# A four-batch retention and Fourier-mixing kernel: the first batch's k read in long runs and transposed twice, under a new written order

## The chip, the cores and the metric

The kernel runs on one core of one Trainium2 chip. The metric is the device time of one execution in microseconds (us), lower is better. Inside the core TensorE multiplies matrices, VectorE, ScalarE and GpSimd do the element-wise work, and SyncE (SP) issues most of the DMAs. Each engine takes its own instructions in a fixed order and waits on semaphores for the others.

## What is computed

Two stages. The first is a recurrent linear attention with a decay per head, the second adds the real part of a two-dimensional Fourier transform, normalises each row, and applies a two-layer network. The cut reference:

```python
# q, k, v: (4 batches, 8 heads, 768 steps, 64) float32
gamma = 1.0 - 2.0 ** (-5.0 - np.arange(H))
for t in range(S):
    state = gamma * state + einsum('bhd,bhe->bhde', k[:, :, t], v[:, :, t])
    y[:, :, t] = 1 / sqrt(D) * einsum('bhd,bhde->bhe', q[:, :, t], state)
x = y.transpose(0, 2, 1, 3).reshape(B, S, H * D)          # (4, 768, 512)

mixed = real(fft(fft(x, axis=1), axis=2))
u = x + mixed
un = (u - mean(u)) / sqrt(var(u) + 1e-06)                  # over the last axis
out = u + maximum(un @ w_ch1, 0) @ w_ch2                   # 512 -> 2048 -> 512
```

## The kernel before

**How the work is cut.** The 768 steps of a head are six chunks of 128. Two heads make a pair, and the four pairs of a batch (taken in the order 0, 1, 3, 2) are one load each of q, k and v: 384 KB in float32, issued by `load_piece` (line 238) on SP. For the first batch q is read as `(p c)`: a partition holds six consecutive steps, which lie next to each other in memory as a run of 1536 bytes. k and v are read as `(c p)`: a partition holds step p of each chunk, in six runs of 256 bytes.

**The first batch, pair i.** `q{i}` casts q to float16 (line 450 and above), `k{i}0` and `k{i}1` cast the two heads of k and multiply with the decay to the end of the chunk (`gkd`), `v{i}0` casts v. `tq{i}` and `tk{i}` transpose q and k on TensorE, six 128x128 transposes each (line 468), `eq{i}` and `ek{i}` copy the result out of PSUM (line 480). As q stands in runs of six steps, `eq` writes with a stride, so that the steps are in order again; `ek` is a plain copy. `am{i}` multiplies the transposed k and q for half of the chunks, `ae{i}` masks the result into `atm` on VectorE (line 505). `kv{i}` multiplies k with v per chunk (line 516), `sc{i}` turns these into the running state with one scan on VectorE (line 529), `yi` and `yx` sum the part within the chunk and the part from the state, and `x{i}0`, `x{i}1` scale the two heads into the tile `x` (line 562).

**From x to the output.** The sequence is folded (`fs`, `fl`, `fh`, `fd`), multiplied with cosine and sine tables (`s1..`), copied out (`gc`, `gr`), multiplied with the tables of the other axis (`s2{kb}` for each of six row blocks), and `qn`, `ul`, `uu`, `xl`, `xu` build u. `bn` and `un` normalise. `ut` transposes a row block, on TensorE or, for later batches, with a transposing DMA on SP. `h` is the first layer into PSUM tiles named `psh` (lines 1101 and 1121; a pool of three), `r` its relu into `ht` (line 1111), `p` the second layer, `o` the last addition and `st` the store. For batches 1 to 3 the names carry the batch in front (`1tq0`, `2un3`, `3h0_1`); there `c..` casts the inputs (`cast_piece`, line 420, all on GpSimd), and r goes to ScalarE or VectorE by a table `ACT_ROWS`.

**What sets the order.** A text `ORDER` lists all units by name, some 1,360 of them, over all four batches. `play` issues them one after the other and `pin` chains each instruction to the one before it on its engine, so that each engine runs its instructions exactly in written order. Units named `f512` are filler matmuls on zeros that nobody reads. A second text, `ENGINES`, says for the first batch's small pieces which engine takes them: P is GpSimd, A ScalarE, D VectorE. The later batches' engines stand in the code. The weights are eight loads on GpSimd's queue (`w10` to `w23`), of which the first is held until the fourth pair's k has landed. Batch 1's first load waits for the seventh weight load and for the matmuls of `h13`.

Of the kernel before, what the change touches and what calls it, by code (L numbers as in the profile page):

```python
# [36 lines left out]
q0:P q1:P q2:P q3:P k00:P k01:P k10:P k11:P k20:A k21:P k30:P k31:A v00:P v10:P v20:A v30:P v31:A  # L37
eq0:D eq1:D eq2:A eq3:A ek00:D ek10:A ek20:A ek30:D ek31:D x00:A x01:A x10:A x11:A x20:A x21:A
x30:A x31:A tn0:D tn1:D tn2:A tn3:D tn4:D gk0:P gk1:A gk2:A gk3:A gc00a:A gc01a:A gc01b:D gc10a:A
gc11a:A gc11b:D ste0:D ste1:A xn0:P xn1:D cdh0:P cdh1:D nsp:P hid5:P fs0a:D fs0b:D fla:D flb:D  # L40
fha:D fhb:D fd0:D fd1:D gr0:P gr1:P gr2:D gr3:D nid0:D nid1:D hid:D
# [3 lines left out]
nid0 lq0 qtz00 lk0 pad01 qtz10 ta0 mp1 hid ta1 gk3 gk1 tn0 mp7 tb0 q0 tq0 tn1 tb1 si1 ab1 f512 mp5  # L45
k00 ab0 k01 tk0 par eq0 co0 ta2 tn2 f512 f512 f512 si0 ek00 am01 nid1 tb2 am00 ae011 ta3 lv0 v00
kv0 ae001 lq1 lk1 lv1 lq2 lk2 q1 tq1 tn3 tb3 k11 f512 f512 gk2 ab2 co2 qz0 si2 si3 ae010 yi01 eq1
gk0 lq3 k10 ae000 tk1 ek10 am10 sc0 lk3 lv2 ab3 yi00 yx0 f512 f512 x01 q2 ae101 v10 am11 ae110
ae111 k20 ae100 tq2 eq2 k21 tk2 ek20 x00 hid5 q3 mp2 kv1 sc1 k31 am21 yi10 nsp k30 am20 w10 w11
w12 ae210 ae201 yi11 yx1 ae200 ae211 tq3 x11 lv3 eq3 tk3 ek30 ek31 f512 ta4 am30 mp3 am31 tn4 tb4  # L50
f512 ae300 ae301 x10 fs0a f512 f512 f512 ae310 v20 kv2 sc2 si4 ab4 yi20 co4 yi21 co3 v31 f512 f512
yx2 v30 kv3 ae311 x20 fs0b s1s10 x21 sc3 flb cdh0 fla co1 fd0 yi31 yi30 yx3 w13 f512 x30 fd1 xn1
x31 xm0 close xm1 s1s00 w20 stx01 fha s1m0 gc00a s1m1 stx3 xn0 fhb s1s11 xmb gc11b gc10a g0a cdh1
s1s01 gc01a gc01b gr1 px1 w21 w22 gc11a gr3 stg00 stx4 stg01 stg10 stg11 stx2 ste1 s22 qn2 ste0
g0b g0c uu2 qe1 s21 qn1 mp0 gr0 ul2 xu2 gr2 uu1 mu1 xm2 mu2 h00 ul1 qz1 h02 un1 h01 s20 qn0 s23
qn3 ul0 xl2 uu0 xu0 s25 ut1 te1 ul3 xl3 h03 uu3 xu3 xl0 bn3 w23 h10 h13 1lk0 1lq0 qn5 uu5 ul5 xu5
un2 s24 qn4 ul4 h12 h11 xl5 ut2 te2 un3 bn5 0p0_1 1lv0 h22 h21 un5 xl4 1lq1 uu4 0p1_1 0p2_1 ut5
h20 ut3 half bn2 qtz01 xu4 bn4 un4 0rt1 1lk1 h23 0p0_0 0p1_0 1cq_0 1lv1 0p2_0 0p3_0 ut4 0p3_1
3ws21 1ck0_0 te5 bn0 te3 1lk2 bn1 0rt0 0rc0 1ck1_0 1tk0 1cv_0 1tq0 te4 1kv0_0 1s0_0 xe 0o1 1kv1_0
1s1_0 1lq2 1ck0_1 1lk3 0o0 1ek_0 0p0_2 1s2_0 1s3_0 1s4_0 0p1_2 0p2_2 1lv2 pad11 1eq1_0 1eq0_0  # L60
1a2_0 1m2_0 mp6 0h1_1 1cq_1 1tq1 1a1_0 0r1_1 1lq3 1eq1_1 1m1_0 0p3_2 0o2 1lv3 1ck1_1 1cv_1 1kv0_1
# [1446 lines left out]
```

## Time and profile before

| | |
|---|---|
| time, median of 3 runs | 239.75 us (238.5 to 240.43) |
| time of the profiled execution | 239.57 us |
| span of the profiled execution, first to last instruction | 237.9 us |
| busy time of VectorE, ScalarE, GpSimd | 190.8, 120.4, 90.9 us |
| DMA | 36.41 MB in 99,466 packets |
| mean granted TensorE clock | 0.993 |

The profile is of one execution. A busy share is time in which an engine has an instruction under way; for TensorE matmuls overlap, so the mean duration of one is longer than the step from one to the next. "Idle before" is the time an engine stood still before the instructions of a group, with what ended the wait. The chain of waits follows the last instruction back to what released it, step by step, and lists start, duration and what it was.

### The profile page before, as it was taken

How to read it: one execution, taken by the hardware profiler on the slowest of the kernel's cores; microseconds unless marked ns; L12 is line 12 of the kernel's file. 1: busy time of each engine (PE TensorE's matmuls, PEld its weight loads, DVE VectorE, ACT ScalarE, POOL GpSimd, SP SyncE). 2: the span in 40 equal slices, each digit the busy share in tenths (PEclk: the TensorE clock that was granted, in tenths of full speed). 3: DMA queues.
4: the chain of work that ended last, by engine and by line, in shares of the span. 5: the costliest groups of instructions: out<-in, count | busy, mean ns of one | idle time of the engine just before them, and what ended most of it. 6: DMA issues, size and time to landing. Idle time of an engine off the chain costs nothing.

```text
span 237.9 us, 5652 instructions
## 1 busy us (share of the span) xinstructions
PE 229.4 (96%) x2175; PEld 159.1 (67%) x2175; DVE 190.8 (80%) x484; ACT 120.4 (51%) x273; POOL 90.9 (38%) x149
## 2 busy tenths in 40 slices
PE   7889999999999999999999999899999999999994
PEld 2456899766776756665667556565666458888884
DVE  7959878878899799886999997987959784856374
ACT  7858875466887543445366334354155316142330
POOL 5667465446640098815404571600004504002302
PEclk9979999999999999999999999999999999999999
DMA  7999999999999999989999968704120240013222
GB/s 178 253 266 179 207 190 151 208 259 233 261 234 232 153 258 180 239 176 155 228 218 252 220 91 154 113 12 101 44 88 3 68 102 8 3 26 111 88 91 88
DMA packets 99466, 36.41 MB, mean 153 GB/s; under 512 B 89840, under 2 KB 96624, under 8 KB 99440
## 3 DMA queue, kind: packets, MB, share of 16 engines
q1 hardware_dynamic: 95072, 31.79, 66.0%
q0 software_dynamic: 4224, 4.19, 11.4%
q8 instruction: 17, 0.28, 0.5%
q14 instruction: 9, 0.07, 0.1%
q10 hardware_dynamic: 144, 0.07, 0.1%
HBM read 27.26 MB, written 6.29 MB: 141 GB/s over the span
## 4 chain that ended last, share of the span: by engine, by line
PE 87%; DMA 4%; DVE 4%; SPq 2%; issue 1%; POOL 1%; ACT 0%; DVEq 0%
PE psc L1146 26%; PE psh L1106 21%; PE psh L1192 8%; PE psc L1242 6%; PE psh L1128 5%; PE wkA L620 3%; PE ps L767 3%; DMA k<-in_k_dram 2%; DMA unT<-un 2%; PE pq L950 2%; PE wkY L679 2%; SPq L244 2%; PE wkY L670 1%; DVE atm L510 1%; PE wkK L643 1%; PE tq L596 1%
## 5 line engine op out<-in xcount | busy, mean ns | idle before, releaser
L1146 PE MATMUL psc<-w,ht 128*128 128x512 f16 x288 | 67.4, 379 | 0.0
L1106 PE MATMUL psh<-unT,w 128*128 128x384 f16 x320 | 59.5, 326 | 0.0
L988 POOL TENSOR_TENSOR u<-u,x 128x256 f32<-128x256 f32 x36 | 23.0, 662 | 69.4 <-DVE u L974 59.2
L1146 PEld LDWEIGHTS <-ht 128*128 128x128 f16 x288 | 27.3, 98 | 27.4
L1106 PEld LDWEIGHTS <-w 128*128 128x128 f16 x320 | 29.7, 98 | 15.4
L1115 ACT ACTIVATE ht<-psh 128x384 f16<-128x384 f32 x46 | 22.2, 490 | 19.1 <-PE psh L1106 18.8
L631 DVE TENSOR_TENSOR atm<-wkA,maskp 128x512 f16<-128x512 f32 x36 | 24.1, 683 | 2.0 <-PE wkA L620 1.7
L1117 DVE TENSOR_SCALAR ht<-psh 128x384 f16<-128x384 f32 x34 | 18.2, 551 | 5.4 <-PE psh L1106 5.3
L1192 PE MATMUL psh<-unT,w 128*128 128x256 f16 x192 | 22.3, 273 | 0.3 <-DMA unT<-un 0.3
L1201 ACT ACTIVATE ht<-psh 128x512 f16<-128x512 f32 x21 | 12.0, 595 | 19.4 <-PE psh L1192 16.6
L224 POOL TENSOR_SCALAR kd<-k,gexp 128x384 f16<-128x384 f32 x30 | 17.5, 591 | 11.0 <-DMA k<-in_k_dram 6.9
L224 POOL TENSOR_SCALAR q16z<-q 128x384 f16<-128x384 f32 (+1 forms) x24 | 14.6, 617 | 18.5 <-DMA q<-in_q_dram 18.0
L1192 PEld LDWEIGHTS <-w 128*128 128x128 f16 x192 | 18.7, 98 | 3.0 <-issue 0.6
L1043 DVE BATCH_NORM_STATS2 bst<-u 128x6 f32<-128x512 f32 x24 | 16.4, 685 | 4.0 <-POOL u L988 2.6
L657 DVE SCALAR_TENSOR_TENSOR s<-s,gk,wkK 128x128 f16<-128x128 f16 x48 | 16.1, 340 | 3.0 <-ACT s L653 1.3
L692 ACT ACTIVATE x<-wkY,gexp 128x384 f16<-128x384 f32 x24 | 13.4, 584 | 10.2 <-PE wkY L679 10.1
L1280 POOL TENSOR_TENSOR u<-u,ws 128x256 f32<-128x256 f32 (+1 forms) x6 | 5.6, 947 | 28.1 <-DVE ws L1280 14.1
L1055 ACT ACTIVATE un<-u,stats 128x512 f16<-128x512 f32 x15 | 10.8, 721 | 8.2 <-DVE stats L1044 3.7
L620 PE MATMUL wkA<-qTz,kT 128*128 128x256 f16 x72 | 13.1, 272 | 0.7 <-DVE stats L1068 0.7
L1153 DVE SCALAR_TENSOR_TENSOR ob<-psc,stats,u 128x512 f32<-128x512 f32 x18 | 13.2, 744 | 0.8 <-PE psc L1146 0.7
L224 POOL TENSOR_SCALAR v<-v 128x768 f16<-128x768 f32 (+1 forms) x15 | 12.5, 833 | 3.3 <-DMA v<-in_v_dram 3.0
L773 ACT CAST g<-ps 128x386 f16<-128x386 f32 x12 | 6.7, 600 | 11.0 <-PE ps L767 10.9
(204 smaller groups left out, 412.0 us busy)
## 6 DMA issues: line engine op xcount, KB each, us to landing
q<-in_q_dram SPq DMA_DIRECT2D x16, 384.0 KB, 6.2
k<-in_k_dram SPq DMA_DIRECT2D x16, 384.0 KB, 5.5
v<-in_v_dram SPq DMA_DIRECT2D x16, 384.0 KB, 6.1
out_dram<-ob SPq DMA_DIRECT2D x18, 256.0 KB, 3.7
w<-in_moe_w_ch_dram POOLq DMA_DIRECT2D x8, 512.0 KB, 8.4
out_dram<-o SPq DMA_DIRECT2D x2, 512.0 KB, 2.8
out_dram<-o SPq DMA_DIRECT2D x3, 128.0 KB, 1.8
unT<-un SPq DMA_TRANSPOSE x15, 2.5
```

Of the source, the lines that this page charges most:

```text
L224: return (nc.gpsimd if e == "P" else nc.vector).tensor_scalar(out=out, in0=in_, scalar1=scale, scalar2=1.0, op0=ALU.mult, op1=ALU.mult)
L620: mm = nc.tensor.matmul(wk[:, c2], st["kT"][:, c, :], st["qT"][:, :, c, :], start=True, stop=True)
L631: nc.vector.tensor_tensor(out=st["atm"][:, 2 * part:2 * part + 2], in0=st["wk", part], in1=maskp[:, PAIR_ORDER[i]].unsqueeze(1).to_broadca ...
L657: nc.vector.scalar_tensor_tensor(out=s16[:, c], in0=s16[:, c - 1], scalar=gk2[:, hp:hp + 1], in1=st["kv", c // 3][:, c % 3], op0=ALU.mult, ...
L988: nc.gpsimd.tensor_tensor(out=u[:, lo:hi], in0=u[:, lo:hi], in1=x[:, 1, 257:1:-1] if n else x[:, 0, 1:257], op=ALU.add)
L1043: nc.vector.bn_stats(bst, lb[b]["u"][:, kb, :])
L1106: nc.tensor.matmul(psh, w116[:, cb, fb * P:(fb + 1) * P], lb[b]["unT"][:, cb, rt * 384:(rt + 1) * 384], start=(cb == 0), stop=(cb == 3))
L1115: nc.scalar.activation(ht16[:, fb, :], psh, AF.Relu, bias=0.0, scale=-1.0)
L1117: nc.vector.tensor_scalar(out=ht16[:, fb, :], in0=psh, scalar1=-1.0, scalar2=0.0, op0=ALU.mult, op1=ALU.max)
L1146: nc.tensor.matmul(lb[b]["psc", rb], ht16[:, fb, rb % 3 * P:rb % 3 * P + P], w216[:, fb, :], start=(fb == 0), stop=(fb == NFB - 1))
L1192: nc.tensor.matmul(psh[:, t], w116[:, cb, fb * P:(fb + 1) * P], lb[B - 1]["unT"][:, cb, p * 256:(p + 1) * 256], start=(cb == 0), stop=(cb ...
L1242: nc.tensor.matmul(pr[key][:, c0:c1], lh(f), rh(f)[:, c0:c1], start=first and f == 0, stop=last and f == 7, skip_group_check=True)
```

## The change

The first batch's k is read like its q, as `(p c)`, six steps per partition in runs of 1536 bytes. One cast of 768 elements per partition takes the place of two of 384 and multiplies with nothing. The result is kept in the unused half of the q tile (`kraw`). `tk` transposes it, and `ek` now writes with a stride, as `eq` does, which gives k transposed with its steps in order (`kT`). Since `kv` needs k with steps on the partitions, new units transpose `kT` back (`kb{i}`, six transposes on TensorE) and copy the result out of PSUM (`eb{i}`). The decay to the end of the chunk goes onto v: two casts, one for each head, each multiplied with `gkd`.

```diff
+KBACK = (0, 1, 2, 3)
@@ load_piece
-            rows = "h (p c) d -> p h c d" if b < NPE and name == "q" else \
-                "h (c p) d -> p h c d"
+            rows = "h (p c) d -> p h c d" if b < NPE and name == "q" or \
+                b == 0 and name == "k" and i in KBACK else "h (c p) d -> p h c d"
@@ k0_unit
+            if i in KBACK:
+                kraw[i] = qzs[i % 2].rearrange("p h c d -> p (h c d)")[
+                    :, NCH * P:2 * NCH * P].rearrange("p (c h d) -> p c h d", c=NCH, h=2)
+                scaled(on[f"k{i}{h2}"], kraw[i], in_of["k", 0, i].rearrange("p h c d -> p c h d"))
+                return
@@ v0_unit
+            if i in KBACK:
+                h = 2 * PAIR_ORDER[i] + part
+                last_cast[0, i] = scaled(on[f"v{i}{part}"], v16_of[0, i][:, :, part], v32[:, :, part],
+                                         gkd[:, h:h + 1])
+                return
@@ t0_unit
-            src = (q16_of, kd_of)[part][0, i]
+            src = kraw[i] if part and i in KBACK else (q16_of, kd_of)[part][0, i]
@@ te_unit
+            elif i in KBACK:
+                scaled(on[f"ek{i}{n}"], st["kT"].rearrange("p c t -> p (c t)").rearrange(
+                    "p (t c) -> p t c", c=NCH), tq.rearrange("p c t -> p t c"))
@@ new
+    def kb_unit(i):
+        def run():
+            st = st_of(0, i)
+            tq = st["tq", 2] = ps_g.tile([P, NCH, P], f16, tag="g", name="tq",
+                                         padded_shape=[P, 8, P])
+            for c in range(NCH):
+                nc.tensor.transpose(tq[:, c, :], st["kT"][:, c, :], ident16)
+        return run
+
+    def eb_unit(i):
+        def run():
+            kd_of[0, i] = kp.tile([P, NCH, 2, D], f16, tag="kd16", name="kd16")
+            scaled(on[f"eb{i}"], kd_of[0, i].rearrange("p c h d -> p c (h d)"),
+                   st_of(0, i)["tq", 2])
+        return run
```

`ENGINES` now names the small pieces of all four batches, and the code asks it for each (`r_piece` as an example; a helper `copied` is new):

```diff
-            if fb in ACT_ROWS[rt]:
+            if on.get(f"{b}r{rt}_{fb}", "A" if fb in ACT_ROWS[rt] else "D") == "A":
...
+    def copied(e, out, in_):
+        if e == "A":
+            return nc.scalar.copy(out, in_)
+        return (nc.gpsimd if e == "P" else nc.vector).tensor_copy(out, in_)
```

Of the 80 relus of batches 0 to 2 in `r_piece`, ScalarE has 67 (46 before) and VectorE 13 (34). Of the 24 of batch 3, ScalarE has 16 (21). Of the 56 input casts of batches 1 to 3, GpSimd keeps 33, ScalarE has 19, VectorE 4. VectorE takes 12 of GpSimd's 36 additions of x in batches 1 to 3 and 17 of ScalarE's 36 copies `q..`. In the first batch the copies `eq` are all on ScalarE (two before), `ek00`, `eb0` and `eb2` are on VectorE, the other `ek` and `eb` on ScalarE; the casts of q1 and the x tiles `x00` and `x01` are on VectorE.

`ORDER` is new from end to end; 24 fillers in all remain, eight of them ahead of the list. Its part up to the first `h` unit (`h02`), the stretch that the prediction follows, and three later stretches that it names:

```diff
+ta1 gk2 gk1 nid1 nid0 hid5 ta0 f512 mp3 lq0 q0 lk0 k00 tq0 lv0 lq1 f512 par tn1 tb1 tn0 eq0 lk1
+k10 mp0 tk0 tb0 ab0 si0 ek00 mp1 q1 v01 lv1 lq2 f512 qtz00 lk2 f512 f512 am01 ae011 lq3 lk3 kb0
+eb0 v10 ta3 si1 lv2 ab1 co1 v11 ta2 v00 am00 f512 tn3 k20 gk0 ae000 tq1 tn2 eq1 ae010 tk1 ek10 tb3
+ae001 tb2 kv0 ab3 kb1 am10 si2 gk3 f512 f512 f512 si3 sc0 yi01 ae101 ab2 yi00 yx0 q2 ae100 eb1 hid
+am11 tk2 ek20 x00 ae111 f512 f512 ae110 x01 tq2 eq2 kv1 sc1 yi11 kb2 eb2 lv3 q3 am21 ae211 yi10
+yx1 k30 tk3 co2 x11 ae210 tq3 am20 ae201 ae200 ek30 x10 fs0a ta4 tn4 w10 w11 eq3 f512 f512 f512
+f512 fs0b v21 kb3 eb3 v20 kv2 yi21 am30 sc2 ae300 w12 tb4 ae301 am31 ae310 ae311 f512 si4 ab4 co4
+co3 yi20 yx2 x21 x20 v30 v31 kv3 s1s10 sc3 stx01 yi31 fla co0 flb xn1 fd0 yi30 yx3 x30 x31 s1s00
+nsp qe1 xm0 cdh0 xm1 fd1 s1m0 gc00a stx3 s1m1 gc10a fha fhb s1s01 xn0 xmb s1s11 qtz01 stg00 stx4
+gc01a gc01b cdh1 gr1 g0a gc11b gc11a g0b g0c xm2 px1 s21 gr3 w13 w20 qn1 ul1 stg01 pad01 stg10
+stg11 mu1 uu1 stx2 gr0 gr2 s23 mu2 s24 ste1 ste0 un1 s22 qz0 qn2 uu2 qtz10 ul2 xu2 close h02 ut1
...
+3q1_3 3u1_3 3ux1_1 2p1_4 3rt0 3bn1 3rc0 3us0 3ut0 2p2_4 3ux0_2 3bn2 3s24 3rt1 3q0_4 3q1_4 3u0_4
+3u0_3 3ux0_3 3q0_5 2p1_5 2p0_3 1st3 3ux1_3 3rc1 2p2_5 2p3_5 3q1_5 3us1 3ux0_4 3u1_4 2o5 3ux1_4
+3u1_5 3ut1 2p3_4 2o4 3rt2 3rc2 3ux1_5 2p1_3 2p2_3 3ws31 3h0_1 3us2 3ut2 3r0_1 3bn3 3rt3 2p3_3 2o3
...
+3ww2_0 3m3a_0 3r1_4 3h1_0 3ww12_0 3r1_3 3r1_0 3h1_6 3m3b_0 3r1_6 3hs20_1 3h1_5 3r1_5 3ut5 3h2_6
...
+2st5 3wc_1 3m2a_1 3m2b_1 3m4a_1 3m4b_1 3hs11_1 3h2_0 3m5b_1 3w7a_0 3r2_3 3m6a_1 3m6b_1 3w5_1 3w2_1
```

In the order before, the units from the copies of the third and fourth pair's x to the first `h` unit (`h00`), and the place of `3us1` and of the last transposes:

```python
yx2 v30 kv3 ae311 x20 fs0b s1s10 x21 sc3 flb cdh0 fla co1 fd0 yi31 yi30 yx3 w13 f512 x30 fd1 xn1
x31 xm0 close xm1 s1s00 w20 stx01 fha s1m0 gc00a s1m1 stx3 xn0 fhb s1s11 xmb gc11b gc10a g0a cdh1
s1s01 gc01a gc01b gr1 px1 w21 w22 gc11a gr3 stg00 stx4 stg01 stg10 stg11 stx2 ste1 s22 qn2 ste0
g0b g0c uu2 qe1 s21 qn1 mp0 gr0 ul2 xu2 gr2 uu1 mu1 xm2 mu2 h00 ul1 qz1 h02 un1 h01 s20 qn0 s23
...
3q0_2 2h1_11 3q1_2 3bn0 3rt0 3u0_2 2p0_4 3ux0_2 3u1_2 3q0_4 3rc0 3us0 2r1_11 3ux1_3 3u0_3 3ux1_1
3bn1 3rt1 3q1_4 2p0_5 2p1_5 3ut0 3rc1 3us1 2p0_3 2p1_3 2p2_5 2p3_5 3ux0_3 3bn3 3rt3 3rc3 3us3 2st1
3ut1 3ux1_2 3bn2 3rt2 3rc2 3us2 2p2_3 2p3_3 2o3 2p1_4 2p2_4 2p3_4 3u0_4 3h0_6 2o5 3q0_5 2o4 3ws20
...
3r1_4 3us4 3ut4 3m6a_0 3m6b_0 3w6_0 2st5 3w2_0 3r1_5 3h1_2 3r1_2 3m5b_0 3w5_0 3ut5 3h1_7 3h1_6
```

More of the change, by code (lines that the diff above doesn't have):

```diff
@@ L36 @@
 ENGINES = """
[L37 to L41, printed above, removed]
+q0:P q1:D q2:P q3:P k00:P k10:P k20:P k30:A v00:A v10:P v20:P v30:P v31:P eq0:A eq1:A eq2:A
@@ L44 @@
 ORDER = """
[L45 to L61, printed above, removed]
@@ L1093, in run @@
             dst, pst = lb[b]["unT"][:, :, kb * P:(kb + 1) * P], lb[b]["pst", kb]
-            if (kb % 2 == 0) != (b == 0 and kb < 3):
-                nc.vector.tensor_copy(dst, pst)
-            else:
-                nc.scalar.copy(dst, pst)
+            e = "D" if (kb % 2 == 0) != (b == 0 and kb < 3) else "A"
+            copied(on.get(f"{b or ''}te{kb}", e), dst, pst)
         return run
```

237 lines of the change are left out of this document (142 added, 95 removed).

## The prediction

> **What bounds the kernel now.** I read the page's first part, then the table of stretches, then the chain of waits. The first row is the page's, the columns of the second fence are the stretch in us, its length, and busy us (with instructions) of each engine, the granted clock, the DMA share and GB/s.
>
> ```profile
> span 237.9 us, 5652 instructions
> ...
> PE 229.4 (96%) x2175; PEld 159.1 (67%) x2175; DVE 190.8 (80%) x484; ACT 120.4 (51%) x273; POOL 90.9 (38%) x149
> ```
>
> ```profile
> 0.00:10.00 10.00, 7.75 (x50) 3.10 (x51) 8.10 (x40) 7.70 (x19) 6.18 (x18) 1.00 0.98 211
> 10.00:20.00 10.00, 8.23 (x122) 5.56 (x119) 7.23 (x15) 6.38 (x14) 7.60 (x12) 0.83 1.27 252
> 20.00:30.00 10.00, 9.67 (x139) 7.41 (x137) 9.07 (x24) 9.14 (x21) 4.73 (x7) 1.00 1.18 187
> 30.00:40.00 10.00, 10.00 (x159) 9.55 (x157) 7.52 (x23) 6.40 (x18) 6.06 (x10) 1.00 1.21 192
> ...
> 150.00:160.00 10.00, 9.31 (x87) 6.10 (x85) 8.87 (x21) 5.07 (x13) 2.38 (x4) 1.00 0.42 67
> ...
> 210.00:220.00 10.00, 9.66 (x89) 8.44 (x88) 6.85 (x18) 2.94 (x7) 1.96 (x2) 1.00 0.29 81
> ```
>
> From 30 us on TensorE has no idle time except 0.69 us in the stretch at 150 and 0.34 us in that at 210: 1.03 us in all. There the time is TensorE's own work, and an edit gains only by taking work from TensorE or by filling those two holes. Before 30 us it is otherwise: TensorE's busy time contains the 24 filler matmuls, and it stands idle for 4.35 us besides. What ends a wait there is a load, a cast or a copy. So I cut the run at the first hidden-layer matmul (L1128); the chain of waits says when that is, and what else I need from it (start, us, what).
>
> ```profile
> 27.08 0.53 PE ps L805 x6
> ...
> 28.85 1.07 PE ps L805 x12
> 29.92 0.45 PE pq L929 x4
> ...
> 31.54 0.44 PE pq L1001 x4
> ...
> 32.64 2.68 PE psh L1128 x48
> ...
> 57.04 0.65 PE psh L1106 x4
> ...
> 63.08 0.34 PE tq L596 x6
> ...
> 213.59 4.98 DMA unT<-un
> ...
> 234.78 0.29 DVE o L1280
> ```
>
> So span = 32.64 us to the first L1128 matmul, 202.14 us from there to the last matmul's reader at 234.78, and 3.12 us of last additions and stores. The profiled execution took 239.57 us, 1.67 us more than its span; the median shown is 239.75, so sums made against the profile stand 0.18 us under the median.
>
> **TensorE's account.** The change adds four units `kb`, each six 128x128 transposes. The row at 63.08 has six such at 0.34 us, so 4 x 0.34 = 1.35 us of new work, all before the cut. Fillers stay 24. Counting units ahead of the first `h` unit in both written orders, the new one also has `s23` and `s24` there, which stood behind it (each four matmuls as in the row at 31.54, 0.44 us). So 0.88 us of the 202.14 moves ahead of the cut and 201.26 is left behind it. With T the new start of the first `h`, span = T + 201.26 + (change in TensorE's holes) + 3.12.
>
> **The loads.** These are GpSimd's casts of the first batch, each with the load that ended its wait in brackets.
>
> ```profile
> 4.10 0.83 POOL L224 TENSOR_SCALAR q16z<-q 128x768 f16<-128x768 f32 x1 [0.46 <-DMA q<-in_q_dram]
> ...
> 5.97 1.15 POOL L224 TENSOR_SCALAR kd<-k,gexp 128x384 f16<-128x384 f32 x2 [1.04 <-DMA k<-in_k_dram]
> ...
> 7.61 0.83 POOL L224 TENSOR_SCALAR v<-v 128x768 f16<-128x768 f32 x1 [0.49 <-DMA v<-in_v_dram]
> ...
> 8.78 0.83 POOL L224 TENSOR_SCALAR q16z<-q 128x768 f16<-128x768 f32 x1 [0.34 <-DMA q<-in_q_dram]
> 10.56 0.58 POOL L224 TENSOR_SCALAR kd<-k,gexp 128x384 f16<-128x384 f32 x1 [0.95 <-DMA k<-in_k_dram]
> ```
>
> All loads are 384 KB and come one after the other. q, in runs of 1536 bytes, follows v after 8.78 - 7.61 = 1.17 us; k, in runs of 256 bytes, follows q after 10.56 - 8.78 = 1.78. Read as q is, each k saves 0.61 us, four of them 2.4 us: k0 is there at 5.3, q1 at 8.2, and everything behind k3 is 2.4 us earlier. The Trainium skill, DMA: Bandwidth & Descriptors, section "Why small descriptors are slow (HBM only)", gives some 3 cycles per packet beside 8 for 256 bytes; by that (an estimate) a k load would take 1.78 x 51/66 = 1.38 us and four would save 1.6, not 2.4. I go by the measured spacing.
>
> **What the new path costs on the other engines** (rows grouped by line and form; count, busy us, mean ns):
>
> ```profile
> L510 DVE SCALAR_TENSOR_TENSOR atm<-wkA,maskf 128x384 f16<-128x384 f32 x16 | 8.2, 548 | 2.5 <-PE wkA L501 2.5
> ...
> L534 DVE TENSOR_TENSOR_SCAN s<-gk,wkK 128x320 f16<-128x320 f32 x4 | 3.3, 814 | 0.8 <-PE wkK L525 0.7
> ...
> L224 DVE TENSOR_SCALAR qTz<-tq 128x768 f16<-128x768 f16 x2 | 1.9, 947 | 0.0
> ...
> L334 DVE MEMSET qTz<- 64x384 uint32 x4 | 1.5, 378 | 0.3
> ...
> L712 DVE TENSOR_TENSOR xab<-x 128x774 f16<-128x774 f16 x2 | 1.1, 552 | 0.0
> ...
> L224 DVE TENSOR_SCALAR kT<-tq 128x768 f16<-128x768 f16 x1 | 0.6, 550 | 0.0
> ```
>
> ```profile
> L223 ACT ACTIVATE kT<-tq 128x768 f16<-128x768 f16 x2 | 1.6, 808 | 1.3 <-PE tq L477 1.3
> ```
>
> - The k cast becomes one of 768 (0.83 on GpSimd, as the q rows) for two of 384 (1.15); the v cast becomes two for one, so the casts cancel. GpSimd has room, since it waits for the loads.
> - The eviction of the transposed k now scatters. On VectorE that is the q form, 0.95 instead of 0.55 (`ek00`); on ScalarE both are 0.81, and the other three stand there.
> - The eviction of the second transpose, `eb`, is new: twice 0.55 on VectorE, twice 0.81 on ScalarE.
> - The decay on v costs nothing: the cast had a scale operand already.
>
> **Which of them ends last.** The first chain is faster: q0 as before, k0 at 5.3 and cast by 6.1 (7.12 before), transposed 6.6, scattered by 7.6 where the old copy ended at 8.73. But then VectorE has a fixed list, in written order, up to the fourth scan `sc3`, and its third item (after `ek00` and `mp1`), the cast of q1, waits for the load of q1 until 8.2. With 0.55 to 0.83 for that cast (a VectorE copy of 768, and GpSimd's) and the 0.38 memset it is about 9.25. From there to the end of `sc3`: 16 `ae` 8.2 us, 4 scans 3.3, two `eb` 1.1, `x00` and `x01` 1.1 (0.55 each, the price of a 128x384 PSUM read by VectorE in the L510 row), two folds 1.1, and `tn2`, `gk0`, `gk3` about 1.1 (less than a 0.55 copy each). Sum 15.9, so `sc3` ends at 25.15 if VectorE never waits. Before:
>
> ```profile
> 25.27 0.82 DVE L534 TENSOR_TENSOR_SCAN s<-gk,wkK 128x320 f16<-128x320 f32 x1
> ```
>
> ```profile
> 26.80 1.05 ACT L223 ACTIVATE x<-wkY,gexp 128x384 f16<-128x384 f32 x2 [0.38 <-PE wkY L557]
> ```
>
> that is 26.09, with the last x at 27.85. The loads offer 2.4 us; VectorE takes 0.94 of it, because the two new evictions, the scatter, q1 and x00, x01 went onto the engine whose 20 to 30 stretch is already busy for 9.07 of 10. I take 0.94: the new transposes lie in TensorE's idle time and the fillers there, hidden as long as VectorE is last; without that cover they cost their 1.35. From the last x to the first `h` the steps are the same (last x 27.85, L805 matmuls until 29.92, first `h` 32.64), plus the 0.88 of `s23`, `s24`: T = 32.64 - 0.94 + 0.88 = 32.58. Bounds of the step: 0 to 2.4.
>
> **TensorE's holes later.** These are what it waited for:
>
> ```profile
> PE wkA L620 <- DVE stats L1068: 0.7, 1, 0.7
> ...
> PE psh L1192 <- DMA unT<-un: 0.3, 1, 0.3
> ```
>
> Both lie where the written order is new. The second belongs to the 4.98 us transpose at 213.59, issued behind an output store on SP; in the new order `3ut5` stands ahead of `2st5`, so that hole can close. But the new distances are short elsewhere: between `3us1` and the first `3h0` stood nine `p` units and stand three now, and what goes between is a transposing DMA, of which the row above took 4.98 us. I count half of the 1.03 us as gained (bounds: all of it, or 2 us more).
>
> Sum: 32.58 + 201.26 - 0.5 + 3.12 = 236.46 span, 1.67 on top: **238.1 us**.
>
> **Rivals.** *VectorE is not the bound early, and the loads' gain goes through.* For it: TensorE waits for GpSimd's casts of k in that stage, and these wait for k. Against: the list above has almost no slack. T = 32.64 - 2.44 + 0.88 = 31.08; with both holes closed the span is 31.08 + 201.26 - 1.03 + 3.12 = 234.43, the time 236.1.
>
> *Casts on ScalarE block the evictions (slower).* Of 56 casts of batches 1 to 3, all GpSimd's, the new list puts 19 on ScalarE and 4 on VectorE, and ScalarE also gets 67 of the 80 relus of 128x384 (VectorE keeps 13 of the 34 below). A cast waits for its load, and the relus queued behind it wait with it, while TensorE has three PSUM tiles for `psh`.
>
> ```profile
> POOL q16z L224 <- DMA q<-in_q_dram: 18.0, 9, 9.5
> ...
> POOL kd L224 <- DMA k<-in_k_dram: 6.9, 6, 1.8
> POOL v L224 <- DMA v<-in_v_dram: 3.0, 4, 1.2
> ```
>
> ```profile
> L1117 DVE TENSOR_SCALAR ht<-psh 128x384 f16<-128x384 f32 x34 | 18.2, 551 | 5.4 <-PE psh L1106 5.3
> ```
>
> GpSimd waited 27.9 us for loads, of which the five rows of the first casts hold 3.3, so at most 24.6/56 = 0.44 us per later cast: 19 x 0.44 = 8.4 us on ScalarE. Two spare tiles cover 2 x 0.65 = 1.3 us (row at 57.04): beyond that a wait is TensorE's. 238.1 + 8.4 - 1.3 = 245.2. It decides from the point at which a load lands more than 1.3 us after ScalarE reaches its cast. Against it: GpSimd's waits show an engine far ahead of its work, and ScalarE, busier, arrives later; 14 of these 19 casts are written 8 us or more of TensorE work behind their loads.
>
> *The gain is used up*: VectorE waits about 1 us more in the first stage for `x` tiles and second transposes, T = 33.5; with the holes as they were the span is 33.5 + 201.26 + 3.12 = 237.9, as now, and the time 239.6. That the loads are not in longer runs can be left out, the access pattern being q's.
>
> **Chances.** A difference of 1% is about what a measurement of this kernel tells from no change, so faster is under 237.35 and slower over 242.15. Forecast 0.44 (of it 0.14 under 237.35, by the bounds of T and the holes), loads go through 0.27 (all faster), ScalarE blocked 0.24 (slower), used up 0.05 (same). Faster 0.41, same 0.35, slower 0.24. The forecast's own range is 236.6 to 239.8. The whole range, 235.0 to 243.5, reaches over the second case and to just short of the third, and leaves out about 2 in 10.
>
> **What would show it.** Right: casts of k0 at about 5.3 and k3's load 2.4 us earlier; VectorE without gaps from 9 to 25 us and the fourth scan ending near 25; the first L1128 matmul near 32.6 with 24 more transposes before it; from there some 201 us with under 1.5 us of idle TensorE. VectorE idle in that stage with T near 31 would show the second case; "ACT ht" or "ACT kd" as releaser of TensorE between 50 and 150 us the third. Wrong altogether: more than 3 us of TensorE holes after the cut, wherever they lie, or DMA of batch 1 late, with TensorE waiting for its casts at 45 to 60 us.

## The result, and the profile after

| | before | after |
|---|---|---|
| time, median of 4 runs each | 239.63 us (238.5 to 240.43) | 242.0 us (241.61 to 242.69) |
| profiled execution, its span | 239.57, 237.9 us | 241.61, 239.7 us |

The ratio is 1.0105, with a 95% interval of 1.0058 to 1.0153: the change makes the kernel about 1% slower. 238.1 had been forecast. Here and below medians are of all executions, while ratios leave out those that took over 1.5% longer than the fastest of their kernel, and so are not quotients of the medians.

From the page of after: span, busy time of the engines, and the row of the DMA queue that brings TensorE's instructions (packets, MB, share).

```profile
span 239.7 us, 5678 instructions
...
PE 232.3 (97%) x2199; PEld 160.5 (67%) x2199; DVE 199.1 (83%) x507; ACT 132.6 (55%) x284; POOL 71.5 (30%) x117
...
q8 instruction: 17, 0.28, 0.5%
```

The table of stretches of after (columns as in the prediction):

```profile
0.00:10.00 10.00, 8.75 (x35) 3.55 (x35) 6.91 (x34) 6.87 (x15) 4.74 (x17) 1.00 0.90 244
10.00:20.00 10.00, 9.56 (x160) 6.71 (x158) 9.51 (x20) 8.66 (x17) 8.46 (x14) 1.00 1.01 242
20.00:30.00 10.00, 9.68 (x139) 7.15 (x139) 9.05 (x23) 9.46 (x24) 6.20 (x9) 1.00 1.22 198
...
120.00:130.00 10.00, 8.31 (x73) 5.88 (x71) 8.51 (x22) 5.24 (x11) 1.76 (x2) 1.00 1.13 220
...
150.00:160.00 10.00, 10.00 (x90) 6.65 (x89) 8.95 (x23) 5.90 (x13) 2.42 (x4) 1.00 0.64 128
...
210.00:220.00 10.00, 10.00 (x94) 8.98 (x92) 8.23 (x21) 2.57 (x5) 1.96 (x2) 1.00 0.21 55
```

The chain of waits of after:

```profile
27.64 1.28 ACT junk L816 x4
28.92 0.50 ACT g L261
...
33.42 0.89 PE psh L1199 x16
...
117.80 4.69 DMA kT<-kd
122.53 0.61 PE wkA L688 x4
...
235.46 1.07 PE psc L1313 x16
```

And the longest of what TensorE waited for in after:

```profile
PE wkA L688 <- DMA kT<-kd: 1.7, 1, 1.7
```

Read with the prediction's sum: L1199 is the first hidden-layer matmul (L1128 before). It comes at 33.42 for 32.64 before, from there to the last matmul's end at 235.46 + 1.07 = 236.53 are 203.11 us, and 3.17 remain. VectorE is busy 9.51 of 10 us between 10 and 20, where it had been 7.23. TensorE's holes at 150 and 210 are closed, and a new one of 1.69 us stands at 120: a transposing DMA of batch 3's k, issued at 117.80, lands 4.69 us later.

### The profile page after: what moved, and what is told of

It is laid out like the page before. It is cut to its first block, busy times and chain, and to the rows that moved or that the text cites. A ratio compares the mean times of both kernels' runs of the same rounds, so it can differ in the third digit from the quotient of the medians.

```text
span 239.7 us, 5678 instructions
## 1 busy us (share of the span) xinstructions
PE 232.3 (97%) x2199; PEld 160.5 (67%) x2199; DVE 199.1 (83%) x507; ACT 132.6 (55%) x284; POOL 71.5 (30%) x117
## 4 chain that ended last, share of the span: by engine, by line
PE 78%; DVE 7%; DMA 5%; ACT 5%; SPq 2%; issue 1%; DVEq 0%; ACTq 0%
PE psc L1217 19%; PE psh L1177 18%; PE psh L1263 9%; PE psc L1313 6%; PE psh L1199 4%; PE wps L252 3%; DMA out_dram<-ob 3%; PE wkA L688 2%; PE ps L834 2%; DMA kT<-kd 2%; DVE atm L699 2%; PE wkY L747 1%; PE tq L525 1%; PE wkY L738 1%; PE pq L1018 1%
## 5 line engine op out<-in xcount | busy, mean ns | idle before, releaser
L1186 ACT ACTIVATE ht<-psh 128x384 f16<-128x384 f32 x67 | 31.6, 493 | 28.8 <-PE psh L1177 28.5
L1177 PEld LDWEIGHTS <-w 128*128 128x128 f16 x320 | 30.0, 98 | 15.8
L1054 POOL TENSOR_TENSOR u<-u,x 128x256 f32<-128x256 f32 x24 | 15.0, 640 | 37.6 <-DVE u L1040 23.2
L1263 PEld LDWEIGHTS <-w 128*128 128x128 f16 x192 | 18.8, 98 | 2.6
L1272 ACT ACTIVATE ht<-psh 128x512 f16<-128x512 f32 x16 | 9.2, 596 | 18.0 <-PE psh L1263 12.9
L262 POOL TENSOR_SCALAR v<-v 128x768 f16<-128x768 f32 x9 | 7.6, 845 | 29.0 <-DMA v<-in_v_dram 21.9
L261 ACT ACTIVATE x<-wkY,gexp 128x384 f16<-128x384 f32 x26 | 14.5, 590 | 1.7 <-PE wkY L747 1.5
L1125 ACT ACTIVATE un<-u,stats 128x512 f16<-128x512 f32 x14 | 10.0, 721 | 6.6 <-DVE stats L1113 5.7
L262 POOL TENSOR_SCALAR q16z<-q 128x384 f16<-128x384 f32 (+1 forms) x13 | 9.7, 749 | 10.0 <-DMA q<-in_q_dram 9.9
L262 POOL TENSOR_SCALAR kd<-k,gexp 128x384 f16<-128x384 f32 x14 | 8.2, 591 | 12.1 <-DMA k<-in_k_dram 7.2
L1199 PE MATMUL psh<-unT,w 128*128 128x128 f16 x192 | 11.5, 219 | 0.0
L1199 PEld LDWEIGHTS <-w 128*128 128x128 f16 x192 | 11.1, 98 | 0.3
```

The lines of the kernel that those rows point to most:

```text
L261: return nc.scalar.activation(out, in_, AF.Copy, bias=0.0, scale=scale)
L262: return (nc.gpsimd if e == "P" else nc.vector).tensor_scalar(out=out, in0=in_, scalar1=scale, scalar2=1.0, op0=ALU.mult, op1=ALU.mult)
L1054: (nc.vector if on.get(f"{b}ux{n}_{kb}", "P") == "D" else nc.gpsimd).tensor_tensor(out=u[:, lo:hi], in0=u[:, lo:hi], in1=x[:, 1, 257:1:-1] ...
L1177: nc.tensor.matmul(psh, w116[:, cb, fb * P:(fb + 1) * P], lb[b]["unT"][:, cb, rt * 384:(rt + 1) * 384], start=(cb == 0), stop=(cb == 3))
L1186: nc.scalar.activation(ht16[:, fb, :], psh, AF.Relu, bias=0.0, scale=-1.0)
L1199: mm = nc.tensor.matmul(psh[:, f], w116[:, cb, fb * P:(fb + 1) * P], unT[:, cb, kb * P:(kb + 1) * P], start=(cb == 0), stop=(cb == 3))
```

## The experiments

Each kernel ran 6 to 12 times, in turn with before, whose medians in the five sets were 239.06 to 239.59; ratios are against before, with 95% intervals. After itself was timed in the first comparison alone, so a difference to it in microseconds compares two sets, and before's medians alone differ by 0.57 us between sets (239.06 to 239.63). "T" is the start of the first hidden-layer matmul's own row in the one profiled execution: 32.48 in before, 33.25 in after.

**hole120: the transposes of batch 3 four groups later.** Do they and the load behind them make the wait at 120?

```diff
-3a2_1 2fs01 2fd01 1st0 3a0_1 3m0_1 2g0a 1h1_7 1h1_11 1r1_7 3a1_1 0st5 1r1_11 2fd00 2fe00 1h1_8
-1r1_8 1h1_5 1r1_5 3m2_1 2fe01
+2fs01 2fd01 1st0 2g0a 1h1_7 1h1_11 1r1_7 0st5 1r1_11 2fd00 2fe00 1h1_8
+1r1_8 1h1_5 1r1_5 3a2_1 3a0_1 3m0_1 3a1_1 3m2_1 2fe01
```

> The changed kernel with one edit in the written order: the score matmuls of batch 3's second pair (3a2_1, 3a0_1, 3a1_1 and the mask 3m0_1) stand four h groups (2.6 us of TensorE) later, so that they come after the transposing DMAs they wait for. Theory A (this hole is time lost on TensorE, and nothing else waits behind it): the 1.86 us wait at 120.5 us goes, time 242.0 - 1.8 = 240.2 us. Rival (what follows in that pair is late anyway, so the wait moves to its y or x units): under 0.5 us gained, 241.5 to 242 us.

241.78 us, 1.009 [1.0062, 1.0119]. What TensorE waited for in hole120:

```profile
PE wkK L711 <- POOL v L262: 1.3, 1, 1.3
```

The wait went from the transposed k to the cast of v, whose load stands behind that transpose on SP and landed at 123.01: the rival's case. So a late consumer alone gains nothing here: both transposes and the load behind them, issued on SP between 114.46 and 117.60, were late.

**old_order: before's order and engines, with the k path put into it by hand.** `kb` and `eb` stand behind each pair's last `am` there. The fourth pair's copy `ek30` goes to ScalarE, and `pad01` moves.

```diff
-am00
+am00 kb0 eb0
...
-am30
+am30 kb3 eb3
```

> The k path alone (long runs, transposed and transposed back, decay on v) in the written order and on the engines of the kernel before, with the second transposes and their copies put in by hand behind the first score matmuls of each pair. Theory A (the later holes belong to the new order, and the k path about pays for itself before the first hidden-layer matmul): holes after the cut as before, 1.5 us, first hidden-layer matmul between 32.0 and 33.0 us, time 239 to 240 us. Rival B (the k path itself is the loss: 24 transposes and four more evictions on full engines): first hidden-layer matmul at 34 us or later, time 241.5 us or more.

243.24 us, 1.0188 [1.0132, 1.0244]. T is 36.56, and the rest runs without holes. Placed without a new order, the path costs some 4 us (243.24 less 239.59 = 3.65 in the time, 4.08 in T), all of it before the first hidden layer. This says what that placement costs, not that none is better.

**no_back: without the transposes and copies back.** The kernel computes v·v where the reference has k·v in the first batch.

```diff
-            kd, v16 = kd_of[0, i], v16_of[0, i]
+            kd, v16 = v16_of[0, i], v16_of[0, i]
...
-kb0 eb0
-kb1
-eb1
-kb2 eb2
-kb3 eb3
```

> The changed kernel without the second transposes and their four evictions; the first batch's state matmuls multiply v with itself in place of k, so the sequence state of batch 0 is another one. Theory A (VectorE is the bound from 10 to 26 us, and two of these evictions, 1.1 us, are in its list): fourth scan ends about 24.6 instead of 25.75 us, time 242.0 - 1.1 = 240.9 us. Rival (the loads or TensorE's tables are the bound there): fourth scan within 0.3 us of 25.75, time 241.7 to 242 us.

239.0 us, 0.9975 [0.9944, 1.0006]: 3.0 under after. `sc3` ends at 24.24, T is 31.62, and there is no wait at 120, though nothing was edited there. So the 3.0 are not the price of the copies in the first stage alone.

**short_runs: the long runs taken away, everything else kept.** k is read in runs of 256 bytes, so the steps come out permuted.

```diff
-                b == 0 and name == "k" and i in KBACK else "h (c p) d -> p h c d"
+                False else "h (c p) d -> p h c d"
```

> The changed kernel with the first batch's k read in runs of 256 bytes again (same work on every engine; k's steps stand in another order, so batch 0 computes with permuted steps of k). Theory A (longer runs brought k3 1.9 us earlier, of which VectorE's list leaves about 0.5 to 1 us): k loads take 1.7 us each again, fourth scan 0.5 to 1.5 us later, time 242.5 to 243.5 us. Rival (the loads' gain goes through in full): fourth scan 2 us or more later, time 244 us. Second rival (the loads were hidden already): no change, 242.0 us.

243.53 us, 1.0166 [1.0129, 1.0204]: the long runs bring 1.5 us. The wait at 120 is still there.

**no_kpath: the new order and engines, k as before.**

```diff
-KBACK = (0, 1, 2, 3)
+KBACK = ()
...
-k00
+k00 k01
...
-kb0
-eb0
...
-v01
```

> The new written order and engines, with the k path as before the change: k in runs of 256 bytes, two casts with the decay, no second transposes, v cast without decay. Theory A (the k path is a net loss: the copies back cost more than the longer runs bring; leaving the copies out was worth 3.0 us and leaving the long runs out cost 1.5 us): 242.0 - 3.0 + 1.5 = 240.5 us, first hidden-layer matmul near 32.7 us. Rival (the new order is the loss and the k path is neutral): 241.5 to 242.5 us.

240.0 us, 1.0026 [1.0012, 1.0039]. The new order by itself costs some 0.6 us, the k path in it 2.0. The largest later hole is one of 0.43 us at 127. So the wait at 120 comes and goes with instructions that run 100 us earlier.

**hole2, warm, both: hole120's move with the load of v further forward and its use later; TensorE kept busy before the first transposes; the two together.**

```diff
-3lv0 3cv_0
+3lv0 3lv1 3cv_0
...
-2fe01 3cv_1 3kv0_1 1rc1 2fe11 1h1_10 1r1_10 1st1 2fe10 3lk2 1h1_3 2g0b
+2fe01 3cv_1 1rc1 2fe11 1h1_10 1r1_10 1st1 2fe10 3lk2 1h1_3 3kv0_1 2g0b
```

> The changed kernel with batch 3's second pair started later: its score matmuls 2.6 us later as in the first edit, its k-times-v matmuls (3kv0_1) 1.3 us later, and the load of its v (3lv1) issued right behind 3lv0, ahead of the transposing DMAs. Theory A (the transposing DMAs and, behind them on the same queue, the v load are late together, and both waits have to be covered): no wait of TensorE over 0.4 us between 100 and 130 us, 1.5 us off the profiled and the median time, 240.3 us. Rival (the wait moves on to the next consumer of that queue): 241.5 us or more.

```diff
-ta1 gk2 gk1 nid1 nid0 hid5 ta0 f512 mp3 lq0 q0 lk0 k00 tq0 lv0 lq1 f512 par
+gk2 gk1 nid1 nid0 hid5 f512 mp3 lq0 q0 lk0 k00 f512 tq0 ta1 ta0 lv0 lq1 par
```

> The changed kernel with two of its fillers put ahead of the first table matmuls, which go behind the first q transposes, so that TensorE works without a gap or a two-row matmul from 1.25 to 5.5 us. Theory C (whether TensorE goes at half pace from 5.5 to 9.5 us differs from execution to execution, and it costs 1.05 us: first hidden-layer matmul 33.25 against 32.2 us in two profiles of the same first part): no transposes at 107 ns behind 6 us, first hidden-layer matmul 32.0 to 32.4 us, median 0.5 to 1 us under that of the changed kernel, 241.0 to 241.5 us. Rival (the pace does not matter, since VectorE or the loads end last): 242 us.

> Both edits (the second pair of batch 3 later with its v load earlier; two fillers ahead of the tables). If both theories hold the gains add: 242.0 - 1.5 - 0.7 = 239.8 us, level with the kernel before. If only one holds: 240.3 to 241.4 us.

hole2: 241.61 us, 1.0082 [1.0051, 1.0114]. warm: 242.5, 1.0116 [1.0085, 1.0146]. both: 241.1, 1.0071 [1.0048, 1.0095]. In hole2 TensorE waited for something else again, at 117.94:

```profile
PE psh L1177 <- DVE ob L1224: 1.0, 1, 1.0
```

That `ob` had itself waited 1.23 us for a store, which now stands behind the load of v on SP.

warm does what it was to do for TensorE's pace (full from 5.0 us) and loses more elsewhere: the granted clock is at half from 25.4 to 28.9 us, and VectorE's two folds of the first pairs' x, 1.03 us in after, take 3.28. They and GpSimd's work beside them:

```profile
20.05 3.28 DVE L779 TENSOR_TENSOR xab<-x 128x774 f16<-128x774 f16 x2
```

```profile
20.18 1.14 POOL L262 TENSOR_SCALAR v<-v,gexp 128x384 f16<-128x384 f32 x2
21.30 1.15 POOL L262 TENSOR_SCALAR ht<-ssp 128x1158 f16<-128x1158 f16 x1
```

The first fold alone lasts 2.81 us, to 22.86, some 0.4 us past the end of GpSimd's three instructions (22.45); the second takes 0.55. T is 34.49.

**narrow8, narrow24, fewer16, before_narrow24: how many instructions TensorE has run before 120 us.** A new theory, called F. TensorE's instructions arrive in 17 blocks of 0.28 MB in all, and the trace shows one such transfer for about every 256 of its matmuls and weight loads (4,398 in 17). In after one comes at 119.71, with the two transposing DMAs under way. If a fetch delays them, a shift in the number of instructions ahead must move the wait, whatever these instructions do. A filler of 512 columns is cut into four of 128: the same work in 6 more instructions.

```diff
-    for _ in range(8):
-        filler(512)()
+    for _ in range(32):
+        filler(128)()
```

> The changed kernel with its eight leading fillers of 512 columns written as 32 of 128: the same TensorE time, 48 more TensorE instructions (a matmul and a weight load each). Theory F (TensorE fetches its instructions in blocks of 16 KB, one per 256 instructions, over the same DMA engines; a transposing DMA in flight when a block is fetched lands some 1.6 us later, and the 24 transposes of the k path moved one such fetch, at 119.7 us, into the transposes for batch 3's second pair): 48 instructions move that fetch by about 1 to 2 us only, to 118.2 to 118.8 us, still inside those transposes (116.3 to 122 us), so the wait at 120 us stays over 1 us, time 241.5 to 242.5 us. Rival (the slow transposes come from the loads and stores around them): the same, 242 us; this kernel is the control for the next.

narrow24 does the same to the 16 fillers of the list (`f512` becomes `f128 f128 f128 f128`), before_narrow24 does both to before; fewer16 takes the 16 out.

> The changed kernel with all 24 fillers written as 96 of 128 columns: the same TensorE time within 0.2 us, 144 more TensorE instructions ahead of 30 us. Theory F: the fetch that fell at 119.7 us falls near 113.5 us, ahead of the transposes of 116.3 us; their landing behind the end of issue is 2.2 and 1.5 us instead of 3.8 and 3.1, the wait of TensorE at 120 us is under 0.3 us, time 242.0 - 1.7 = 240.3 us (other fetches then fall at 128 and 144 us, into transposes that need not be on the path). Rival (loads and stores around): the wait stays, 242 us.

> The changed kernel without the 16 fillers of the written order: 32 TensorE instructions fewer. Theory F: the fetch of 119.7 us falls at 122 us or later, behind those transposes, and the wait at 120 us is under 0.3 us, time 240.3 us if the fillers lay in idle time and the clock holds without them. Rival: the wait stays, and the clock, with 3.4 us less work before 30 us, drops to half pace there: first hidden-layer matmul over 34 us, 243 us.

> The kernel before with all 24 fillers written as 96 of 128 columns: 144 more TensorE instructions, the same work. Theory F (the two late holes of that kernel, 0.86 us at 153.7 and 0.50 us at 218.1 us, stand behind transposes that were in flight at the fetches of 152.3 and 216.1 us): both holes under 0.2 us, other transposes hit (near 114, 128 and 144 us), time between 238.1 and 239.4 us according to whether those are on the path. Rival: holes as they are, 239.4 us.

narrow8: 241.45 us, 1.008 [1.0055, 1.0105]. narrow24: 240.6, 1.0028 [1.0, 1.0057]. fewer16: 241.69, 1.006 [1.0025, 1.0096]. before_narrow24: 238.97, 0.9999 [0.9976, 1.0023].

The fetch moves with the count: 119.71 in after, 117.08 in narrow8 (48 instructions more, in an execution that is some 2 us earlier at that point), 111.31 in narrow24 (144 more), 121.27 in fewer16 (32 fewer). In all 19 profiles the tenth fetch comes when TensorE has started 2,463 to 2,525 matmuls and weight loads, though its time is anywhere from 109 to 124 us. The two transposes as SP issues them, in after and in narrow24 (start, us to issue):

```profile
116.26 1.45 SPq L650 DMA_TRANSPOSE qTz<-q16z  x1
117.80 1.62 SPq L654 DMA_TRANSPOSE kT<-kd  x1
```

```profile
116.09 1.45 SPq L650 DMA_TRANSPOSE qTz<-q16z  x1
117.63 1.57 SPq L654 DMA_TRANSPOSE kT<-kd  x1
```

The same time of issue within 0.2 us; what the tile's view says of the landing of k's, first in after, then in narrow24:

```profile
DMA to landing us min/median/max: 4.7/4.7/4.7
```

```profile
DMA to landing us min/median/max: 3.1/3.1/3.1
```

And what the DMAs did meanwhile, in single microseconds (last two columns: DMA share and GB/s), in after and in narrow24:

```profile
119.00:120.00 1.00, 1.00 (x23) 0.77 (x20) 0.96 (x3) 1.00 (x3) 0.00 (x0) 1.00 1.36 214
120.00:121.00 1.00, 0.84 (x6) 0.29 (x3) 0.86 (x3) 0.84 (x3) 0.00 (x0) 1.00 1.74 11
121.00:122.00 1.00, 0.00 (x0) 0.00 (x0) 0.94 (x2) 0.36 (x1) 0.00 (x0) 1.00 0.75 163
```

```profile
119.00:120.00 1.00, 1.00 (x22) 0.77 (x20) 0.97 (x3) 0.28 (x1) 0.00 (x0) 1.00 1.12 216
120.00:121.00 1.00, 1.00 (x18) 0.68 (x15) 1.00 (x3) 1.00 (x3) 0.00 (x0) 1.00 0.45 99
```

In after 11 GB/s flow in the microsecond behind the fetch, with packets under way all through it (the share is not zero), and TensorE (first column of busy time) falls to nothing in the next. narrow24 has no wait there, though its transfers thin out to 99 GB/s too. narrow8, with the fetch still among the transposes, keeps its wait (its view of waits):

```profile
PE wkA L688 <- DMA kT<-kd: 1.6, 1, 1.6
```

The other profiles of the new order settle it, since they all have these two transposes, issued in 1.43 to 1.45 and 1.53 to 1.66 us. In seven (after, hole120, hole2, warm, both, short_runs, narrow8) a fetch comes between the issue of q's and the landing of k's, and k's lands 4.58 to 4.77 us after its issue starts, q's 5.25 to 5.54. In the other eight it does not, and k's lands after 3.11 to 3.17 us, q's after 3.68 to 3.79. No value lies between. no_back belongs to the eight: with 48 instructions fewer its fetch came at 121.13, behind k's landing at 118.34. So of the 3.0 us by which it is under after, some 1.7 are this wait. T's 1.63 there are not all the copies' price: hole120 and hole2, with the copies, are only 0.6 and 0.4 us above no_back's T.

before_narrow24 agrees: both late holes of before are gone. They stood behind transposes issued at 149.3 and 213.6 us, with fetches at 152.3 and 216.0; for the first the profile names VectorE's `stats`, which ended 0.13 us after that transpose had landed. Its time stays; in the profiled execution T was 33.2 instead of 32.48. There the first fetch, at 17.14 in before, fell at 14.37, into the loads: the fourth q landed at 17.70 instead of 16.21. Its clock was at half from 7.4 to 10.8 us besides. fewer16 missed F's number: its fetch came behind the transposes, which were on time, and fell on the next transfer, the load of v (its view of waits):

```profile
PE wkK L711 <- POOL v L262: 1.5, 1, 1.5
```

In its profiled execution the granted clock was full only from 14.1 us on and at half again from 24.3 to 27.7, which is what its rival had feared, and T was 33.69. One profile does not show that the missing fillers did it.

**combo, combo_v3, before_combo, combo_v4, nok_v4: is there a version that gains?** narrow24 also had T = 34.29, with folds of 2.37 us. combo is narrow24 with warm's edit; before_combo puts both into before. combo_v3 and combo_v4 also move GpSimd's work away from the folds, and nok_v4 has combo_v4's moves, with fillers of 512 and no k path. The edits of combo_v3 (the first two) and of combo_v4 (all four):

```diff
-sc2 ae300 w12 tb4
+sc2 ae300 v30 v31 w12 tb4
...
-x21 x20 v30 v31 kv3
+x21 x20 kv3
...
-ta4 tn4 w10 w11
+ta4 tn4 nsp w10 w11
...
-s1s00 nsp qe1
+s1s00 qe1
```

> The changed kernel with both settled edits: all 24 fillers as 96 of 128 columns (the fetch of 119.7 us moved out of the transposes) and eight of these ahead of the first table matmuls. Theory: no wait over 0.4 us between 105 and 125 us; TensorE at full pace from 5.3 us; first hidden-layer matmul 31.6 to 32.2 us where VectorE's two folds take 1.0 us, 33 to 34.5 us where they take 2 us or more. Time 238.0 to 238.5 us without, 239.5 to 240.5 us with such folds, median between. Rival (the pace and the fetch are not what bounds it): median as with the narrow fillers alone, 240.6 us or more.

> As combo, with GpSimd's last two v casts ahead of its third weight load's issue, so that GpSimd has a stretch without element-wise work while VectorE folds. Theory D (VectorE's folds and GpSimd's casts keep each other waiting, and a fold that loses waits until GpSimd is free of such work): the two folds take at most 1.7 us, the runs near 240 us become fewer, median 238.0 to 238.8 us, under that of the kernel before. Rival (the slow folds have another cause, or the later weight load costs as much): median as combo.

> The kernel before with all 24 fillers as 96 of 128 columns and eight of these ahead of its first table matmul. Theory: its two late holes stay closed (1.35 us); at full pace early its first hidden-layer matmul is at 32.3 to 32.6 us: 238.0 to 238.5 us. Rival (TensorE's pace before 10 us is hidden behind the loads there, and the narrow fillers bring nothing): 239.0 to 239.3 us.

> As combo_v3, with GpSimd's sign change of a sine table (128x1158, 1.15 us) moved ahead of its first weight load's issue, so that after its v casts GpSimd has nothing but the issue of a weight load until 24 us. Theory D (a fold of VectorE that finds GpSimd at element-wise work waits until GpSimd is free of it; in combo_v3 it waited 1.5 us until the sign change ended): the two folds take at most 1.6 us, first hidden-layer matmul at 33 us or earlier, median 238.0 to 238.8 us, under that of the kernel before. Rival (the folds are slow for another reason): folds of 2 us or more again, median 240 us.

> The new order without the k path, with the fillers ahead of the tables and GpSimd's casts and sign change moved as in combo_v4, but its fillers of 512 columns kept, since its fetches fell clear of the transposes at 120 us. Theory (in the first stage the longer runs bring 1.5 us and the copies back cost 0.5 to 1 us): first hidden-layer matmul 0.5 to 1 us later than in combo_v4, median 238.8 to 239.6 us. Rival (the copies back cost as much as the runs bring): medians of the two within 0.3 us.

combo: 240.3 us, 1.0027 [1.0, 1.0055]. combo_v3: 240.21, 1.0028 [0.9998, 1.0058]. before_combo: 238.91, 0.9992 [0.9971, 1.0014]. combo_v4: 239.24, 1.0006 [0.9987, 1.0025]. nok_v4: 239.91, 1.0028 [1.0011, 1.0045].

combo_v3's edit was not enough: its folds took 2.56 us and ended 0.9 us behind the sign change (`nsp`, the 128x1158 row above). With `nsp` away too, in combo_v4:

```profile
20.45 1.30 DVE L780 TENSOR_TENSOR xab<-x 128x774 f16<-128x774 f16 x2
```

Its T is 32.5. combo_v4 takes back the 2.8 us that after stands above it without touching the k path, and is level with before. nok_v4 is 0.7 us slower than combo_v4 in the same set. That may be what the k path is worth there, but the two intervals overlap, and the fillers differ too. No version is measurably faster than before.

## Why the prediction was wrong

Its sum was 32.58 + 201.26 - 0.5 + 3.12; measured were 33.42 + 203.11 + 3.17. The time lay in the range, but it rose where a fall had been forecast. The miss of 3.24 us in the span is 0.84 in T, 2.35 in the holes, 0.05 in the tail.

**TensorE's account: right.** At 216 ns from start to start for 512 columns, as both traces show, the matmuls of after cost 1.30 us more than before's (1.35 forecast), 0.86 us of work moved ahead of the cut (0.88 forecast), and the holes below explain the rest of the stretch behind the cut to within 0.02 us.

**The loads: right in kind.** k follows q after 1.06 to 1.13 us (1.17 forecast). The estimate from the Trainium skill, DMA: Bandwidth & Descriptors, section "Why small descriptors are slow (HBM only)", 1.38, does not hold here. But the last k landed 1.93 us earlier, not 2.4: the second q came 2.28 us after the first v, where it had been 1.17 (8.90 instead of the 8.2 I had used). Why was not traced; in hole120 and hole2, the same program up to 100 us, it came 1.81 and 1.43 us after that v, so it differs from execution to execution. short_runs puts the worth of the long runs in the whole time at 1.5 us.

**VectorE's list: its length right, its start wrong.** VectorE's timeline of after (start, us, what, then idle time before it), from the scattered copy `ek00` to the list's first `ae`, and the fourth scan:

```profile
8.20 0.96 DVE L262 TENSOR_SCALAR kT<-tq 128x768 f16<-128x768 f16 x1 [1.67 <-PE tq L525]
9.08 0.22 DVE L262 TENSOR_SCALAR maskp<-maskf 128x128 f32<-128x128 f32 x1
9.21 0.55 DVE L262 TENSOR_SCALAR q16z<-q 128x768 f16<-128x768 f32 x1
9.78 0.38 DVE L372 MEMSET qTz<- 64x384 uint32 x1
10.15 0.56 DVE L577 SCALAR_TENSOR_TENSOR atm<-wkA,maskf 128x384 f16<-128x384 f32 x1
...
24.93 0.82 DVE L601 TENSOR_TENSOR_SCAN s<-gk,wkK 128x320 f16<-128x320 f32 x1
```

The list took 25.75 - 10.15 = 15.6 us (15.9 forecast), from 10.15 instead of 9.25. The load of q1 at 8.90 alone would have made it 8.90 + 0.55 + 0.38 = 9.83. The rest is `ek00`, forecast to end at 7.6, which ended at 9.16 behind its transposes, although k's cast was done at 6.0, as forecast:

```profile
5.17 0.83 POOL L262 TENSOR_SCALAR q16z<-k 128x768 f16<-128x768 f32 x1
```

TensorE was slow there. Six transposes of 128 columns in before's timeline, then in after's, q and k:

```profile
5.87 0.50 PE L477 MATMUL tq<-ident,q16z 128*128 128x128 f16 x6
```

```profile
5.93 0.85 PE L525 MATMUL tq<-ident,q16z 128*128 128x128 f16 x6
...
7.32 0.84 PE L525 MATMUL tq<-ident,q16z 128*128 128x128 f16 x6
```

In after they start 107 ns apart, in before 55: the trace's list of the granted clock begins, at full, at 9.9 us in after and at 4.6 in before. So `sc3` ended at 25.75 (25.15 forecast, 26.09 before). From there to T it took 7.67 us (7.43 forecast), the rest mostly ScalarE's `junk` sums ahead of the `g` copy in the chain. The list had no slack, as the prediction said, so the late start went through to T. The third rival, given 0.05, had the size (T = 33.5), but another cause: waits for `x` tiles and second transposes. The step is not refuted as such: hole120 and hole2, the same program up to 100 us, ended `sc3` at 24.70 and 24.48 in their profiled executions, with T 32.20 and 31.98, better than forecast. But those executions took 239.9 and 240.1 us, where the medians of their kernels are 241.78 and 241.61.

**TensorE's holes later: the step that failed.** It counted half of 1.03 us as gained. Both old holes went, and more came. By the time between starts of successive matmuls, less 216 ns for each 512 columns, the stretch behind the cut has 6.68 us of holes for 4.82 before: 1.86 more. The step's bound had allowed 2 us more; the term in the sum was 0.5 less. A single one of 1.86 us, at 120.5, accounts for it; what closed (0.86 and 0.50 at 153 and 218) and what else opened (0.34 at 65.6, 0.37 at 95.3 and many small ones) cancel. The prediction had named a short distance to a transposing DMA in batch 3's end as the danger; it came at batch 3's start, and not through a distance. "More than 3 us of holes after the cut" had been the mark for wrong altogether, and 6.68 by starts (some 2 us by idle time) shows that the mark lacked a definition.

What the step left out is the instruction fetch on top of the two DMAs: the fifteen profiles above show it for this wait. The step could not have been sized from before's row at 213.59 without asking why that transposition took 4.98 us where the median of its kind on after's page is 2.4: a fetch came in the middle of it. Of the 2.0 us that the k path costs in the new order (no_kpath against after), I put most on this wait: narrow24, which cuts the fillers and so moves the fetch, is 1.4 under after, and 0.85 under narrow8 in its own set.

**The rivals.** That the loads' gain goes through did not happen: VectorE was the bound. ScalarE's casts do not block: it waits for the load of a cast once for 3.0 us and once for 0.2, and no wait of TensorE in after names a cast of ScalarE. ScalarE's view of waits:

```profile
ACT kd L261 <- DMA k<-in_k_dram: 3.0, 1, 3.0
```

**What stays open.** Why a fetch stalls other DMAs; why q1's load came late; what decides when TensorE's clock is first granted in full. T of the fifteen profiles of the new order lies between 31.6 and 34.8 us, and differs by 1.3 between profiles of the same first part (after and hole2), so a T from one profile can support a median but not replace it.

## What to carry to other kernels

A saving in the first stage is worth only what the engine with the full list there leaves of it, and that list's start must be taken from its latest input, not from the mean spacing of loads. Adding instructions to an engine shifts when its later instruction blocks are fetched: if a new wait appears far from the edit, behind a transposing DMA, compare the times of fetch and issue before rewriting anything there, and try the same work in another number of instructions. Test such an order change in parts, with medians of many runs.

## What the runs showed of the hardware

**Instruction fetches and DMAs.** The two transposes issued at 114 to 120 us land 1.4 to 1.9 us later with one of TensorE's fetches beside them, in seven profiles against eight. Over all 19 profiles, with the fetches of every engine counted, the transposing DMAs of k landed a median of 1.56 us after their issue had ended where no fetch began between issue and landing (76), and 2.64 where one did (76); of q 2.25 (84) and 3.23 (68), of the normalised rows 1.24 (225) and 1.88 (60). Longer transfers meet more fetches, so these medians alone prove nothing; the two transposes do not have that bias. Ordinary loads are hit too, as the load of v in fewer16. A fetch is not the only cause of a thin stretch: of 430 stretches of at least 0.7 us (in steps of 0.1) under 25 GB/s with a transfer outstanding, 123 began within 1.7 us behind one of TensorE's fetches. The Trainium skill, Runtime: NRT & Kernel Launch, section "Instruction fetch mechanics", gives blocks of 256 instructions on a queue of their own, which the row of q8 bears out, and calls the cost of crossing one mostly hidden; here one crossing came with a hole of 1.86 us.

**VectorE beside GpSimd.** The same two folds took 1.03 us in after, 1.30 in combo_v4 and 3.28 in warm. The Trainium skill, SBUF — State Buffer, section "SBUF: two separate sides", says that a VectorE operation with two inputs from SBUF and a GpSimd operation that reads SBUF exclude each other for a whole instruction. The lengths agree with that, and warm adds that the loser can sit out several instructions in a row (20.18 to 22.45).

**TensorE's pace and the granted clock.** TensorE begins at half pace: in after its first fillers of 512 columns start 427 ns apart, later ones 216. The trace's own list of the granted clock has its first entry, at full, at 9.9 us in after, at 4.6 in before, and at 4.1 and 5.2 in hole120 and hole2, which are the same program as after up to 100 us; there the half pace ends. The tables of stretches read 1.00 wherever that list has no entry, so the 1.00 in after's first row says nothing. T is 33.25 in after, 32.20 in hole120 and 31.98 in hole2. A lapse later costs too: before's own executions with a mean granted clock under 0.998 took longer, in every set, by 0.6 to 0.9 us (239.82 for 238.99 in the first, 11 and 12 runs). The profiled one, with half the clock from 14.8 to 18.3 us (0.83 in the row of 10 to 20), is of that kind, so the prediction's sum started from a lapse; the four of after all had 0.998 or more.
